# Chunks 1 and 2 take their four tiles as one group of 512 columns in the second mixer, its first matrix a pair ahead, and the planner counts port waits in the tails

## The chip, the core and the metric

The kernel runs on one core of one Trainium2 chip. The metric is the time of the whole kernel on the device, in microseconds (us). Before the change three runs gave 1989.48, 1990.63 and 1990.86 us; the median is 1990.63 us.

The engines are named here as the profile names them: PE is TensorE (PEld its weight loads), DVE is VectorE, ACT is ScalarE, POOL is GpSimd, SP is the engine that issues most of the DMAs.

## The reference, cut to what matters

One sequence of S = 2048 rows, D = 512 columns, H = 32 heads, F = 1792 hidden columns.

```python
mod = silu(c) @ w_mod                      # six rows of 512: sa, ca, ga, sb, cb, gb
h = layernorm(x) * (1 + ca) + sa
x = x + ga * attention(h, wqkv, wo)        # 32 heads of 16 columns
h = layernorm(x) * (1 + cb) + sb
# block B on h:
u = gelu(layernorm(h) @ w1)                # shifted by +1, -1, +2, -2 rows, a quarter of the columns each
x1 = h + shifted(u) @ w2                   # first mixer, across rows
B = x1 + gelu(layernorm(x1) @ w3) @ w4     # second mixer, across columns
out = x + gb * B
```

## The kernel before

The work is cut into four **chunks** of 512 rows, each of four **tiles** of 128 rows. First come the weights and q, k and v, then the attention, chunk by chunk, which takes three quarters of the time. After it, or between its last steps for chunk 0, each chunk runs a **tail**: the output projection `wo`, two layer norms, `w1` with GELU, `w2` with the row shift, another layer norm, and then the second mixer, `w3` with GELU and `w4`.

Every fp32 product is made of three matmuls: each operand is split into a high part and a low part, and high x high, high x low and low x high are added in PSUM (lines 356, 358, 360). A block of 128 output columns of `w3` thus takes 4 x 3 = 12 matmuls, whose moving side is as wide as the group of rows that they serve. A tile of `w4` takes 3 matmuls of 512 columns for each 128 hidden columns.

**Groups.** The shift by up to two rows means that a chunk can finish its `w2` only for rows whose followers are there, so that chunk 0 carries three tiles into the second mixer, chunks 1 and 2 the last tile of the chunk before and three of their own, and chunk 3 five. The list `sub` holds these tiles in groups. Chunk 0 has one group of three tiles (384 columns), chunks 1 and 2 have two groups of two (256 columns each), chunk 3 has a group of two and a group of three.

**Plans.** `PLAN` says in which order the pieces of `w3` and `w4` come. In `PAIRS` (chunk 0) a piece is 256 hidden columns, called a pair, and `w3` runs one pair ahead of `w4`. In the other plan (chunks 1 to 3) `w3` takes four blocks of 128 columns, then `w4` takes the same four.

**Weights.** Each piece of 1 MB holds both parts of the split weights. Chunk 0 builds the pieces of `w3` and `w4` itself (`fresh`, lines 1217 to 1219): a piece is loaded raw in two halves; POOL multiplies it by `gb` (`w4` alone), ACT rounds the high part, DVE subtracts for the low part (`wr<-raw,wr`). It is stored to DRAM, and later chunks load it back (`wr<-Ws`). A `Ring` gives out a few buffers in order.

**Order.** The whole program is one list of instructions per engine, written in the order in which a planner issues them. `Sched` keeps a clock for each engine; a chain of operations on ACT, DVE and POOL is put on these clocks by its costs (`cA`, `cD`, `cG` for 512 columns and so on), and generators (`tail`, `rest` for the second mixer, `norm_T` for the transposes of a normalised group) give their matmuls to PE when the planner's clock says that what they need is ready. Generators earlier in the list go first: the tails of chunks 1 to 3 stand before the second mixers. On the chip each engine then follows its own list strictly, so an instruction that is issued too early holds up what stands behind it.

The names in the profile: `xT` is a bank of transposes, from `osb` (attention output), `xf` (normalised for `w1` in chunks 1 to 3) or `xn` (the same in chunk 0, and normalised for `w3` in all chunks); `A` holds the split transposes; `g` the GELU results; `sq` the buffer between GELU and its split; `trs` the reciprocal root that POOL computes for a layer norm; `x` and `xb`/`xbs` the tiles of the residual. `w<-A,wr` is `w1` or `w3`, `w<-wr,g` is `w2` or `w4`.

Of the kernel before, what the change touches and what calls it, by code (L numbers as in the profile page):

```python
# [8 lines left out]
F32 = mybir.dt.float32  # L9
# [6 lines left out]
OP = mybir.AluOpType  # L16
# [5 lines left out]
P = 128  # L22
# [3 lines left out]
NC = S // CH  # L26
# [79 lines left out]
XB = 4  # L106


class Sched:
# [41 lines left out]
    def put(self, e, cost, ready, fn):  # L151
        self.end = self.T[e] = max(self.T[e], ready) + cost
        fn()
        return self.end
# [164 lines left out]
def cD(n=CH):  # L319
    return n / 0.96 + 69  # L320
# [7 lines left out]
def kernel(ctx, tc, A_x, A_wqkv, A_wo, B_w1, B_w2, B_w3, B_w4, c, w_mod, out):  # L328
# [869 lines left out]
    def fresh(w, i, key):  # L1198
        nm = pieces[i][0]
        left = [2]  # L1200

        def one(f):
            raw.append(f)
            left[0] -= 1
            if not left[0]:
                done.add(key)
                sch.dma(dma.dma_start, Ws[i], w.bitcast(F32))
                if len(made) == len(order["w3"] + order["w4"]) and len(raw) == NRAW:
                    raw.clear()
                    rings["r"].add([0])  # L1210
        for c in range(2):
            yield lambda: (i, c) in loadedq
            f, e = loadedq.pop((i, c))
            hi, lo = [w[:, h, 512 * c:512 * c + 512] for h in range(2)]
            ops = []
            if nm == "w4":
                ops.append(("G", cG(), lambda f=f: pool.tensor_tensor(f, f, gbrow, op=OP.mult)))
            sch.chain(*ops, ("A", cA(), lambda f=f, hi=hi: act.activation(hi, f, AF.Copy)),
                      ("D", cD(), lambda f=f, hi=hi, lo=lo: dve.tensor_tensor(lo, f, hi, op=OP.subtract)),
                      (None, 0, partial(one, f)), ready=e, prio=FPRIO)  # L1220
# [6 lines left out]
    PLAN = [PAIRS, [(nm, i, f0, nf) for i, (f0, nf) in enumerate(FG) for nm in ("w3", "w4")]]  # L1227
# [63 lines left out]
    def tail(ci):  # L1291
# [3 lines left out]
        if ci > 1:  # L1295
            yield lambda: ("w1", ci - 1) in done
# [71 lines left out]
        def ln_apply(dst, src, rs, mv):  # L1368
            return ("D", cD(), lambda: dve.tensor_scalar(dst, src, mv[:, 0:1], rs[:, 0:1], op0=OP.subtract, op1=OP.mult))
# [27 lines left out]
        def norm_T(ts, key, i):  # L1397
# [4 lines left out]
            xlive[xtag(key, ts[0])] -= len(ts)  # L1402

        for i, t in enumerate(new):
# [21 lines left out]
            go = partial(sch.chain, ("D", cD(), x1_add), ("D", 1050 + 750, center), ("D", 750, scale), *ops2,  # L1426
# [6 lines left out]
        def gelu(b, n, hi, lo, key):  # L1433
# [3 lines left out]
            sq = fa.tile([P, 3 * P], F32, name="sq", tag="sq", bufs=XB)[:, :n]  # L1437
# [63 lines left out]
        w, more = ring.get(2)  # L1501
        for si, ts in enumerate(sub):
            yield lambda: all(("g", ci, i, n) in done for i in range(1 + (t0 + 1 in ts)) for n in range(4))
            for t in ts:
# [10 lines left out]
                z = (("D", cD(), lambda xb=xb: dve.tensor_tensor(xb, xb, gbrow, op=OP.mult)),  # L1515
# [6 lines left out]
        if ci == 0:  # L1522
            rings["r"] = Ring(MIXER[0] + MIXER[1] * (NC - 1), rings["0"].spare)
            yield lambda: "C" in done
        sch.add(rest(ci, sub, An, gelu, wait_bank, tG))

    def rest(ci, sub, An, gelu, wait_bank, tG):
# [3 lines left out]
        plan = PLAN[ci > 0]  # L1531
        g2 = {}
        for nm, fi, f0, nf in plan:
# [3 lines left out]
            if nm == "w3":  # L1537
                g2[fi] = [tG(si, len(ts) * P, fi % 2 * nf if not ci else 0) for si, ts in enumerate(sub)]
# [202 lines left out]
```

## Time and profile before

| what | value |
|---|---|
| median of three runs | 1990.63 us |
| the profiled execution, its own time | 1992.18 us |
| its span (first to last instruction) | 1990.4 us |
| PE busy | 1934.7 us, 97% |
| DVE, ACT, POOL busy | 79%, 73%, 77% |
| attention ends, tails alone from | about 1509 us |
| chunk 0 done with its second mixer | about 1657 us |
| chunk 1, chunk 2, chunk 3 done | about 1772, 1889 and 1987 us |

Busy PE is the time in which at least one matmul was under way; a matmul of 512 columns is shown as 0.39 us long though the next one starts 0.23 us after it. How fast PE works is therefore read from the starts of a row of matmuls, and where it loses time from the column of idle time before an instruction, which names who ended it.

### The profile page before, as it was taken

The numbers are of one execution on the slowest core, as the hardware profiler recorded it, in microseconds if no ns is written. First come the engines' busy times: TensorE is split into PE (matmuls) and PEld (weight loads), VectorE is DVE, ScalarE is ACT, GpSimd is POOL, SyncE is SP. The second block draws the span as 40 slices with busy tenths as digits, with TensorE's granted clock in tenths as the row PEclk, the third lists the DMA queues.
The fourth block names the chain that finished last, engine by engine and source line by source line (L and its number), as shares of the span: only waits on it lengthen the run. The fifth ranks groups of instructions, "written<-read, shape, count | busy, mean of one in ns | idle before, by whom it ended". The sixth has DMA issues, their size and how long they took to land.

```text
span 1990.4 us, 41169 instructions
## 1 busy us (share of the span) xinstructions
PE 1934.7 (97%) x14456; PEld 1160.1 (58%) x14456; DVE 1579.6 (79%) x2763; ACT 1453.7 (73%) x2940; POOL 1535.6 (77%) x1404
## 2 busy tenths in 40 slices
PE   7999999999999999999999999999999989999999
PEld 5755554554444444444444444444457879898998
DVE  6398888888999999999999999999976784425211
ACT  6438887778999999999999999999975423232222
POOL 6339998889999999999999999999994653334222
PEclk9989999999999999999999999999999999999999
DMA  8777666454534353535353535364514766553541
GB/s 292 236 197 189 155 175 185 126 136 125 104 73 109 73 109 73 109 73 109 73 108 74 109 73 109 73 162 104 107 40 176 287 226 251 220 199 123 204 150 69
DMA packets 185502, 277.95 MB, mean 140 GB/s; under 512 B 117104, under 2 KB 127856, under 8 KB 169008
## 3 DMA queue, kind: packets, MB, share of 16 engines
q1 hardware_dynamic: 181792, 267.20, 49.5%
q10 hardware_dynamic: 2304, 4.20, 0.6%
q0 software_dynamic: 1200, 3.93, 0.5%
q8 instruction: 114, 1.87, 0.4%
q14 instruction: 92, 0.75, 0.1%
HBM read 211.81 MB, written 62.91 MB: 138 GB/s over the span
## 4 chain that ended last, share of the span: by engine, by line
PE 75%; DVE 13%; ACT 4%; issue 3%; DMA 3%; POOL 2%; SPq 0%; ACTq 0%; POOLq 0%; DVEq 0%
PE mb L992 17%; PE sc L1019 12%; PE pv L1093 11%; DVE mx L988 10%; PE w L356 6%; PE w L360 6%; PE w L358 6%; PE pv L1090 5%; PE ot L1120 3%; ACT pt L1015 3%; DMA wst<-in_A_wqkv_dram 1%; PE xT L1254 1%; POOL pt L1068 1%; DMA wr<-Ws 1%; PE q L360 1%
## 5 line engine op out<-in xcount | busy, mean ns | idle before, releaser
L988 DVE TENSOR_REDUCE mx<-mb 128x1 f32<-128x512 f32 x2048 | 1250.5, 681 | 57.0 <-PE mb L992 51.8
L1068 POOL TENSOR_SCALAR pt<-pt 128x1024 f16<-128x1024 uint16 x772 | 1017.0, 1368 | 67.3 <-ACT pt L1015 66.4
L1015 ACT ACTIVATE pt<-sc 128x512 int32<-128x512 f32 x1688 | 890.4, 623 | 94.7 <-PE mb L992 70.7
L992 PE MATMUL mb<-kst,qtl 62*128 62x512 f32 x2048 | 785.4, 463 | 17.4 <-ACT pt L1015 8.6
L1019 PE MATMUL sc<-qtl,kst 64*128 64x512 f32 x2048 | 744.0, 450 | 2.8 <-DVE mx L988 1.8
L992 PEld LDWEIGHTS mb<-kst,qtl 62*128 62x128 f32 x2048 | 361.6, 193 | 260.4 <-ACT pt L1015 137.8
L1019 PEld LDWEIGHTS sc<-qtl,kst 64*128 64x128 f32 x2048 | 337.3, 185 | 188.4 <-DVE mx L988 118.3
L1093 PE MATMUL pv<-pt,vst 128*32 128x512 f16 x3376 | 318.0, 395 | 3.6 <-ACT ac L1110 3.6
L1453 POOL TENSOR_TENSOR g<-sq,g 128x256 fp32r<-128x256 f32 (+1 forms) x120 | 95.3, 796 | 178.1 <-ACT g L1452 169.8
L1450 ACT ACTIVATE sq<-w 128x256 f32<-128x256 f32 (+1 forms) x126 | 51.4, 408 | 236.5 <-PE w L360 235.6
L1068 POOL TENSOR_SCALAR xbs<-xbs 128x1024 f16<-128x1024 uint16 x165 | 219.3, 1362 | 4.5 <-ACT xbs L1015 4.5
L1015 ACT ACTIVATE xbs<-sc 128x512 int32<-128x512 f32 x360 | 199.9, 642 | 10.9 <-PE mb L992 8.5
L1093 PEld LDWEIGHTS <-vst 128*32 128x32 bf16 x4096 | 91.2, 94 | 180.8 <-issue 162.0
L1560 DVE TENSOR_TENSOR x<-x,w 128x512 f32<-128x512 f32 x73 | 49.7, 684 | 156.7 <-PE w L360 156.7
L1090 PE MATMUL pv<-pt,vst 128*32 128x512 f16 (+1 forms) x1688 | 172.1, 391 | 1.6 <-POOL pt L1068 1.6
L358 PE MATMUL w<-A,wr 128*128 128x256 f32 (+1 forms) x520 | 155.1, 298 | 1.1 <-DVE A L346 1.0
L356 PE MATMUL w<-A,wr 128*128 128x256 f32 (+1 forms) x520 | 155.5, 299 | 0.2 <-DMA wr<-Ws 0.2
L360 PE MATMUL w<-A,wr 128*128 128x256 f32 (+1 forms) x520 | 154.6, 298 | 0.0
L356 PE MATMUL w<-wr,g 128*128 128x512 f32 x270 | 106.6, 395 | 2.0 <-DMA wr<-Ws 2.0
L358 PE MATMUL w<-wr,g 128*128 128x512 f32 x270 | 106.3, 394 | 0.0
L360 PE MATMUL w<-wr,g 128*128 128x512 f32 x270 | 106.2, 393 | 0.0
L358 PEld LDWEIGHTS w<-A,wr 128*128 128x128 f32 x520 | 100.2, 193 | 3.0 <-DVE A L346 2.1
(173 smaller groups left out, 2295.9 us busy)
## 6 DMA issues: line engine op xcount, KB each, us to landing
wr<-Ws SPq DMA_DIRECT2D x66, 1024.0 KB, 5.5
vst<-Vs SPq DMA_DIRECT2D x64, 768.0 KB, 5.2
kst<-Ks SPq DMA_DIRECT2D x126, 384.0 KB, 6.0
Ws<-wr SPq DMA_DIRECT2D x14, 1024.0 KB, 5.2
qtl<-Qs SPq DMA_DIRECT2D x128, 96.0 KB, 4.1
Vs<-vt SPq DMA_DIRECT2D x32, 384.0 KB, 4.3
Ks<-qk SPq DMA_DIRECT2D x16, 512.0 KB, 4.1
Qs<-qk SPq DMA_DIRECT2D x16, 512.0 KB, 3.0
```

Of the source, the lines that this page charges most:

```text
L356: te.matmul(o, lh, rh, start=first, stop=False)
L358: te.matmul(o, lh, rl, start=False, stop=False)
L360: te.matmul(o, ll, rh, start=False, stop=last)
L988: end = sch.crit("D", 605, e + PX, lambda: dve.reduce_max(mxs[u][:, j, g, c:c + 1], b, axis=AX.X))
L992: return ready, lambda: te.matmul(b, lhs, kst[u % 3][r, c * CH:(c + 1) * CH], start=True, stop=True), after
L1015: ea = sch.crit("A", 480, e + PX, lambda: act.activation(pt[s][:, j], b, AF.Exp))
L1019: return ready, lambda: te.matmul(b, kst[u % 3][r, kt * P:(kt + 1) * P], qst[u][r], start=True, stop=True), after
L1068: e_low[s] = XP["G"] + sch.crit("G", 1345, ready, lambda: pool.tensor_scalar(o, i, 0.5, 1.0, op0=OP.mult, op1=OP.mult))
L1090: te.matmul(acc[r:r + n, :], v[:, kt + i, c:c + n].bitcast(F16), pt[s + i].bitcast(F16)[:, j, 0::2], start=False, stop=kt == NKT - 2, skip ...
L1093: te.matmul(acc[r:r + 32, :], v[:, kt, r:r + 32], pt[s].bitcast(F16)[:, j, 1::2], start=kt == 0, stop=False, skip_group_check=True)
L1120: te.matmul(b[:, t * n:(t + 1) * n], ac[:, t * P:(t + 1) * P], smat.rearrange("p j d -> p (j d)"), start=True, stop=True)
L1453: ("G", cG(n), lambda: pool.tensor_tensor(lo, sq, hi, op=OP.subtract)), (None, 0, end), bank=b)
```

## The change

- `sub` for chunks 1 and 2 is one group of four tiles, so that a block of `w3` is 12 matmuls of 512 columns; each group is transposed when all four of its tiles are normalised.
- `PLAN` gives chunks 1 and 2 the order `PAIRS`; chunk 3 keeps its plan.
- The buffers between a GELU and its split (`sq`) become 512 columns wide, and three in number where there were four.
- The tail of a chunk after the first starts when the chunk before it has taken its `w2` pieces and two pieces wait in the ring, where it started at the end of the `w1` of that chunk.
- Costs of some DVE operations with SBUF operands (`Shared`: the low part of fresh weights, the two steps of a layer norm, the multiplication by `gb`) are put on the DVE clock behind the last POOL operation, if that started before them.

```diff
-XB = 4
+XB = 3
+class Shared(float):
+    pass
...
     def put(self, e, cost, ready, fn):
-        self.end = self.T[e] = max(self.T[e], ready) + cost
+        t = max(self.T[e], ready)
+        if e == "G":
+            self.busyG = t, t + cost
+        elif isinstance(cost, Shared) and self.busyG[0] <= t:
+            t = max(t, self.busyG[1])
+        self.end = self.T[e] = t + cost
...
-                      ("D", cD(), lambda f=f, hi=hi, lo=lo: dve.tensor_tensor(lo, f, hi, op=OP.subtract)),
+                      ("D", Shared(cD()), lambda f=f, hi=hi, lo=lo: dve.tensor_tensor(lo, f, hi, op=OP.subtract)),
...
-    PLAN = [PAIRS, [(nm, i, f0, nf) for i, (f0, nf) in enumerate(FG) for nm in ("w3", "w4")]]
+    PLAN = [PAIRS] * (NC - 1) + [[(nm, i, f0, nf) for i, (f0, nf) in enumerate(FG) for nm in ("w3", "w4")]]
...
         if ci > 1:
-            yield lambda: ("w1", ci - 1) in done
+            yield lambda: ("w2w", ci - 1) in done and len(rings["f"].q) >= 2
...
-            sub = [[t0 - 1, t0], new[1:3 + end]]
+            sub = [[t0 - 1, t0], new[1:3 + end]] if end else [[t0 - 1] + new[:3]]
...
-            return "x4" if ci and t in sub[0] else "xn"
+            return "x4" if ci and t in sub[0][:2] else "xn"
...
-            go = partial(sch.chain, ("D", cD(), x1_add), ("D", 1050 + 750, center), ("D", 750, scale), *ops2,
+            go = partial(sch.chain, ("D", cD(), x1_add), ("D", Shared(1050 + 750), center), ("D", Shared(750), scale), *ops2,
...
-            sq = fa.tile([P, 3 * P], F32, name="sq", tag="sq", bufs=XB)[:, :n]
+            sq = fa.tile([P, 4 * P], F32, name="sq", tag="sq", bufs=XB)[:, :n]
...
-        plan = PLAN[ci > 0]
+        plan = PLAN[ci]
```

Up to the last steps of the attention the instructions stand as before on PE. From there they are in another order, and three places show how.

The first is PE's list where chunk 2 goes from `w1` to `w2`, before:

```order
L356 MATMUL w1_26257<-A_24576,wr_26040 128x256
L358 MATMUL w1_26257<-A_24576,wr_26040 128x256
L360 MATMUL w1_26257<-A_24576,wr_26040 128x256
L356 MATMUL w2_26276<-wr_26042,g1_24441 128x512
L358 MATMUL w2_26276<-wr_26042,g1_24441 128x512
```

and now (the `w3` is that of chunk 1):

```order
L370 MATMUL w1_26199<-A_24525,wr_25985 128x256
L368 MATMUL w3_26140<-A_7629,wr_25847 128x512
L370 MATMUL w3_26140<-A_7629,wr_25847 128x512
L366 MATMUL w3_26140<-A_7629,wr_25847 128x512
L368 MATMUL w3_26140<-A_7629,wr_25847 128x512
L370 MATMUL w3_26140<-A_7629,wr_25847 128x512
L366 MATMUL w3_26227<-A_7629,wr_25847 128x512
L368 MATMUL w3_26227<-A_7629,wr_25847 128x512
L370 MATMUL w3_26227<-A_7629,wr_25847 128x512
L366 MATMUL w2_26233<-wr_25987,g1_24464 128x512
L368 MATMUL w2_26233<-wr_25987,g1_24464 128x512
```

Eight matmuls of `w3`, 512 columns wide, now stand between the last of `w1` and the first of `w2`.

The second place is PE's list where chunk 0's tiles, normalised for `w3`, are transposed (`xT<-ident,xn`), before:

```order
L360 MATMUL wo_24828<-wr_24580,A_24576 128x512
L1254 MATMUL xT_24858<-ident_64,xn_7631 128x128 x3
L1254 MATMUL xT_24863<-ident_64,xn_7631 128x128 x3
L1254 MATMUL xT_24870<-ident_64,xn_7631 128x128 x3
L1254 MATMUL xT_24876<-ident_64,xn_7631 128x128 x3
L356 MATMUL w3_24889<-A_7629,wr_24775 128x384
L358 MATMUL w3_24889<-A_7629,wr_24775 128x384
```

and now:

```order
L370 MATMUL wo_24872<-wr_24529,A_24525 128x512
L1264 MATMUL xT_24914<-ident_64,xn_7631 128x128 x3
L1264 MATMUL xT_24927<-ident_64,xn_7631 128x128 x3
L1264 MATMUL xT_24935<-ident_64,xn_7631 128x128 x3
L1264 MATMUL xT_24942<-ident_64,xn_7631 128x128 x3
L366 MATMUL w1_24960<-A_24525,wr_24612 128x256
L368 MATMUL w1_24960<-A_24525,wr_24612 128x256
```

Chunk 0's `w3` followed the transposes; now the `w1` of chunk 1 does. Between the `w2` of chunk 0 and the `w2` of chunk 1 stood 93 matmuls of `w3` and 36 of `w4` of chunk 0, and now stand 38 and none; the others follow later.

The third place is DVE's list up to the second `xf` of chunk 2, which the transposes of that chunk's first two tiles need, before:

```order
L1421 SCALAR_TENSOR_TENSOR xbs_7630<-x1_25445,tmv_25591,cbrow_77 128x512
L1424 SCALAR_TENSOR_TENSOR xbs_7630<-xbs_7630,trs_25592,sbrow_62 128x512
L367 BN_STATS tst_25593<-xbs_7630 128x6
L368 BN_AGGR tmv_25594<-tst_25593 128x2
L1361 TENSOR_SCALAR tmv_25594<-tmv_25594 128x1
L1560 TENSOR_TENSOR x1_22200<-x1_22200,w4_25705 128x512
L1219 TENSOR_TENSOR wr_25660<-raw_23997,wr_25660 128x512
L1369 TENSOR_SCALAR xf_7632<-xbs_7630,tmv_25594,trs_25595 128x512
```

and now:

```order
L1432 SCALAR_TENSOR_TENSOR xbs_7630<-x1_25280,tmv_25415,cbrow_77 128x512
L1572 TENSOR_TENSOR x1_22202<-x1_22202,w4_25479 128x512
L1572 TENSOR_TENSOR x1_22552<-x1_22552,w4_25498 128x512
L1435 SCALAR_TENSOR_TENSOR xbs_7630<-xbs_7630,trs_25416,sbrow_62 128x512
L1229 TENSOR_TENSOR wr_25507<-raw_23997,wr_25507 128x512
L377 BN_STATS tst_25417<-xbs_7630 128x6
L378 BN_AGGR tmv_25418<-tst_25417 128x2
L1371 TENSOR_SCALAR tmv_25418<-tmv_25418 128x1
L1572 TENSOR_TENSOR x1_22200<-x1_22200,w4_25547 128x512
L1229 TENSOR_TENSOR wr_25546<-raw_23997,wr_25546 128x512
L1229 TENSOR_TENSOR wr_25507<-raw_23997,wr_25507 128x512
L1379 TENSOR_SCALAR xf_7632<-xbs_7630,tmv_25418,trs_25419 128x512
```

Two subtractions for fresh weights and additions of `w4` results have moved in front of this `xf`.

## Rows read from the trace of the kernel before

**Rows 1.** The head of the page: the span.
```profile
span 1990.4 us, 41169 instructions
```
**Rows 2.** Windows; stretch: length, then busy by engine, clock, DMA share, GB/s.
```profile
1514.07:1593.30 79.23, 74.28 (x415) 66.61 (x415) 55.38 (x97) 34.08 (x70) 39.06 (x43) 0.94 0.73 266
1593.30:1656.80 63.50, 55.84 (x272) 48.86 (x273) 51.38 (x80) 18.93 (x36) 32.09 (x29) 0.95 0.70 253
1656.80:1764.20 107.40, 106.88 (x686) 96.91 (x685) 39.08 (x73) 31.34 (x76) 39.54 (x55) 1.00 0.57 210
```
**Rows 3.** Timeline of PE, chunk 1's mixer: start, length, engine, line, operation.
```profile
1713.39 0.27 PE L356 MATMUL w<-A,wr 128*128 128x256 f32 x1
...
1724.77 0.28 PE L360 MATMUL w<-A,wr 128*128 128x256 f32 x1
1724.89 0.39 PE L356 MATMUL w<-wr,g 128*128 128x512 f32 x1
...
1735.65 0.39 PE L360 MATMUL w<-wr,g 128*128 128x512 f32 x1
```
**Rows 4.** Timeline of PE: the first weights of `w2`, chunks 2 and 3.
```profile
1692.38 0.40 PE L360 MATMUL w<-wr,g 128*128 128x512 f32 x1
1693.30 0.50 PE L356 MATMUL w<-wr,g 128*128 128x512 f32 x1 [0.52 <-DMA wr<-Ws]
...
1817.40 0.50 PE L356 MATMUL w<-wr,g 128*128 128x512 f32 x1 [0.58 <-DMA wr<-Ws]
```
**Rows 5.** Groups by line, 1600 to the end: count, busy us, mean ns.
```profile
L1560 DVE TENSOR_TENSOR x<-x,w 128x512 f32<-128x512 f32 x67 | 45.6, 685 | 156.5 <-PE w L360 156.4
L1453 POOL TENSOR_TENSOR g<-sq,g 128x384 fp32r<-128x384 f32 x15 | 16.2, 1079 | 17.2 <-ACT g L1452 13.4 <-issue 3.8
```
**Rows 6.** Waits of PE, 1510 to 1660: total us, times, longest.
```profile
PE xT L1254 <- DVE xf L1369: 8.6, 3, 7.2
PE xT L1254 <- DVE sq L1444: 1.8, 1, 1.8
PE xT L1254 <- DVE xn L1369: 1.8, 1, 1.8
PE w L358 <- DVE A L346: 1.0, 2, 0.7
```
**Rows 7.** Timeline of PE: the longest of these waits.
```profile
1639.54 1.76 PE L1254 MATMUL xT<-ident,xf 128*128 128x128 f32 x7 [7.20 <-DVE xf L1369]
```
**Rows 8.** Timeline of DVE and POOL: a DVE operation beside POOL, and others alone.
```profile
1560.60 1.28 POOL L1217 TENSOR_TENSOR raw<-raw,gbrow 128x512 f32<-128x512 f32 x1
1560.68 1.48 DVE L1369 TENSOR_SCALAR xf<-xb,tmv,trs 128x512 f32<-128x512 f32 x1
1562.09 0.68 DVE L1219 TENSOR_TENSOR wr<-raw,wr 128x512 fp32r<-128x512 f32 x1
...
1564.29 0.54 DVE L1369 TENSOR_SCALAR xf<-xb,tmv,trs 128x512 f32<-128x512 f32 x1
```
**Rows 9.** Groups by line on DVE, 1514.07 to 1656.8: count, busy us, mean ns.
```profile
L1219 DVE TENSOR_TENSOR wr<-raw,wr 128x512 fp32r<-128x512 f32 x28 | 26.0, 942 | 0.4 <-ACT wr L1218 0.3
L1424 DVE SCALAR_TENSOR_TENSOR xb<-xb,trs,sbrow 128x512 f32<-128x512 f32 x4 | 4.8, 1194 | 0.0
L1369 DVE TENSOR_SCALAR xf<-xb,tmv,trs 128x512 f32<-128x512 f32 x4 | 3.4, 854 | 0.7 <-POOL trs L1364 0.7
L1424 DVE SCALAR_TENSOR_TENSOR xbs<-xbs,trs,sbrow 128x512 f32<-128x512 f32 x2 | 3.2, 1590 | 0.4 <-POOL trs L1364 0.4
L1369 DVE TENSOR_SCALAR xf<-xbs,tmv,trs 128x512 f32<-128x512 f32 x2 | 2.6, 1323 | 0.0
```
**Rows 10.** Windows: stretches at half clock (the clock stands third from the end).
```profile
1514.70:1518.00 3.30, 3.30 (x18) 3.30 (x17) 1.58 (x4) 2.16 (x5) 0.00 (x0) 0.50 0.99 413
1545.40:1552.20 6.80, 6.31 (x19) 5.80 (x20) 6.66 (x15) 1.65 (x3) 3.77 (x4) 0.50 0.75 261
1637.60:1644.30 6.70, 4.76 (x18) 4.76 (x19) 5.51 (x8) 2.34 (x4) 3.01 (x2) 0.50 0.82 289
```

More of the change, by code (lines that the diff above doesn't have):

```diff
@@ L120, in __init__ @@
         self.end = 0.0
+        self.busyG = 0.0, 0.0
         self.gapmin = GAPMIN
@@ L1368, in ln_apply @@
         def ln_apply(dst, src, rs, mv):
-            return ("D", cD(), lambda: dve.tensor_scalar(dst, src, mv[:, 0:1], rs[:, 0:1], op0=OP.subtract, op1=OP.mult))
+            return ("D", Shared(cD()), lambda: dve.tensor_scalar(dst, src, mv[:, 0:1], rs[:, 0:1], op0=OP.subtract, op1=OP.mult))
         def later(key, fn):
@@ L1401, in norm_T @@
             yield from transposed(lambda k, j: xn[key, ts[j]][:, k * P:(k + 1) * P], range(KT), len(ts), A)
-            xlive[xtag(key, ts[0])] -= len(ts)
+            for t in ts:
+                xlive[xtag(key, t)] -= 1
         for i, t in enumerate(new):
@@ L1501, in tail @@
         w, more = ring.get(2)
+        done.add(("w2w", ci))
         for si, ts in enumerate(sub):
@@ L1514, in tail @@
                 r, m, ops = ln_ops(xb)
-                z = (("D", cD(), lambda xb=xb: dve.tensor_tensor(xb, xb, gbrow, op=OP.mult)),
+                z = (("D", Shared(cD()), lambda xb=xb: dve.tensor_tensor(xb, xb, gbrow, op=OP.mult)),
                      ("G", cG(), lambda xb=xb, x1=x1: pool.tensor_tensor(x1, x1, xb, op=OP.add)), mark(("z", t)))
@@ L1522, in tail @@
         if ci == 0:
-            rings["r"] = Ring(MIXER[0] + MIXER[1] * (NC - 1), rings["0"].spare)
+            rings["r"] = Ring(sum(MIXER, []), rings["0"].spare)
             yield lambda: "C" in done
@@ L1537, in rest @@
             if nm == "w3":
-                g2[fi] = [tG(si, len(ts) * P, fi % 2 * nf if not ci else 0) for si, ts in enumerate(sub)]
+                g2[fi] = [tG(si, len(ts) * P, fi % 2 * nf if plan is PAIRS else 0) for si, ts in enumerate(sub)]
                 for si, ts in enumerate(sub):
```

## The prediction

> **What bounds the kernel now.** I read the page first, then the windows by stage, then the timeline of PE (TensorE), and last what PE waited for. The span is 1990.4 us [rows 1], the profiled execution took 1992.18 us, and the median of the runs is 1990.63 us. My sum is made against the profiled execution, and the forecast is set against the median, 1.55 us lower. Up to the last steps of the attention PE's list is unchanged, so that only the time from about 1500 us on can change.
>
> There, two stages differ. While chunk 0 is in its tail and second mixer (1514.07 to 1656.8), the windows show PE idle for 5.0 us of 79.2 and 7.7 us of 63.5, and the clock at 0.94 and 0.95, while VectorE is busy for 55.4 and 51.4 us [rows 2]. In the mixer of chunk 1 the clock is 1.00 and PE is idle for 0.5 us of 107.4 [rows 2]. So in chunks 1 to 3 a matmul less is time saved, and in chunk 0 what counts is what PE waits for: VectorE, for 8.6 + 1.8 + 1.8 + 1.0 = 13.2 us [rows 6]. The longest wait, 7.2 us, is that of the transposes for chunk 2 [rows 7].
>
> **Wider matmuls in chunks 1 and 2.** 96 matmuls of 256 columns start from 1713.39 to 1724.77, 95 steps, 0.1198 us each; 48 of 512 columns from 1724.89 to 1735.65, 47 steps, 0.2289 us each [rows 3]. In each of the two chunks `w3` has 14 blocks x 12 matmuls x 2 groups = 336 of 256 columns; now 168 of 512. Over both, 672 x 0.1198 = 80.5 us become 336 x 0.2289 = 76.9 us: **-3.6 us**, and no other engine covers it, since PE sets the pace there. As bounds for the new shape I take the rows of the same width in `w4` and a tenth either way of the gain: -4.0 to -3.2.
>
> The Trainium skill, "TensorE: Matmul & The Clock Gate", section "Back-to-back issue gap", gives a fixed 2.5 ns for each matmul on top of its columns; 336 matmuls fewer would be worth 0.84 us by that, an estimate from the page. The rows give 2 x 119.8 - 228.9 = 10.7 ns for the second matmul, and I keep them.
>
> What else goes with it costs nothing. The plan in pairs adds 3 more turns of `w4` in each chunk over 4 tiles, 24 additions of 0.685 us [rows 5] or 16.4 us of VectorE over two chunks; VectorE has 39 us of work in 107 [rows 2], and each addition stands beside the 6 matmuls (1.37 us) of the next tile. The GELU of a block is now 512 wide: POOL took 1.08 us for 384 [rows 5], so some 1.4 us for 512, against 12 x 0.229 = 2.75 us in which PE makes the next block. Three buffers hold 8.2 us of blocks; that one buffer is gone is not felt while a chain takes less than that. Without this cover POOL would set the pace, which is far off.
>
> **A DMA wait that is covered.** The first `w2` of chunk 2 starts 0.92 us after the matmul before it, where 0.23 is the rule: it waits 0.69 us for its weights [rows 4]. Now eight `w3` matmuls, 1.83 us, stand in front: **-0.7 us**. The like wait in chunk 3 [rows 4] stays, as its `w2` still follows `w1` directly. Bounds -0.7 and 0.
>
> **Chunk 0 in another order.** PE's work here is the same; it is cut differently. 55 `w3` and 36 `w4` matmuls, about 17.8 us, move from before the `w2` of chunk 1 to behind it. I go through the waits, first with VectorE as slow as now. 384 columns I price at 0.174 us, halfway between the two steps above.
> - First transposes after the attention: 1.8 us [rows 6]. The normalised tile now stands behind splits of the other transposes, two to four operations of about 0.68 [rows 8], with 11 matmuls of `wo` in front: 1.8 to 4.5, I take 2.9.
> - Transposes of chunk 0 for `w3`, and the split after them: 1.8 + 1.0 [rows 6]. In front stood 28 matmuls of `wo` after the last `w2`, now 20, that is 1.8 us less cover: 4.6, at most 6.5 with the operations that have moved in front on VectorE.
> - First transposes for chunk 1: 1.4 (the 8.6 less the 7.2). PE's cover goes from 60 `w3` and 18 `w4` (14.6 us) to 48 `w1` and 16 `w3` (8.5 us); VectorE's list loses 3 subtractions for weights, 2 statistics, a centring, a scaling and 2 additions, some 7.6 us. Depending on whether PE runs at half clock there, 0 to 4.1; I take 2.3.
> - Transposes for chunk 2: 7.2 [rows 7]. VectorE's list from the second addition of `wo` to the `xf` gains 2 subtractions (0.94 each [rows 9]) and an addition, +2.6; PE's cover goes from 36 `w4` and 38 `w3` to 37 and 49, +2.1: 7.7.
>
> That makes 17.5 us against 13.2. Now the planner's new rule. Beside a POOL operation that ends at 1561.88, an `xf` takes 1.48 us; alone it takes 0.54, and a subtraction 0.68 [rows 8]. Over the stage the subtractions lose 28 x 0.26 = 7.3 us in this way, `xf` 2.8 and the scaling (against 0.68) 3.9: 14.0 us [rows 9]. If the planner's clock knows all of it, it gives the transposes to PE later, with other matmuls in front; if it knows nothing, all stays. It counts VectorE behind the last POOL operation, and not POOL behind VectorE, so I take half, 7 us: 10.5 us against 13.2, **-2.7 us**, with +4.3 and -9.7 as ends. Last, 24 matmuls of `w1` (2.9 us) that stood between the last steps of the attention now follow it: +0.5, from 0 to 2.9.
>
> The Trainium skill, "SBUF — State Buffer", section "Who interferes with whom", has VectorE and GpSimd share a pair of ports as an exclusive lock: whoever starts first holds it to the end of the instruction. Rows 8 agree for VectorE's side. By that rule POOL is late as often, which the planner's rule leaves out; this speaks for the second rival.
>
> **Sum.** -3.6 - 0.7 - 2.7 + 0.5 = -6.5 us: 1985.7 for an execution like the profiled one, **1984.1** for the median.
>
> **The rivals.**
> 1. *The waits nearly go.* With all 14 us known to the planner the waits are 3.5 us: -3.6 - 0.7 - 9.7 + 0.5 = -13.5, or 1977.1; one of the spells at half clock, 6.8 us long [rows 10], would go with them, 3.4 us more: 1973.7. I put it at 1975.5. For it: VectorE is busy for 107 of 143 us [rows 2], so that there is room. Against it: all four waits stand behind long runs of VectorE work, where there is nothing else to give to PE. Chance 0.20.
> 2. *The planner's rule changes nothing on the chip* and the 17.5 us stay: -3.6 - 0.7 + 4.3 + 0.5 = +0.5, or 1991.1, no change that can be told. For it: the counts of VectorE's list above. Chance 0.22.
> 3. *Slower: VectorE becomes the bound of the first stretch and PE's clock falls.* The first stretch loses 17.8 us of PE's work, and with it the cover. After each of three waits the clock fell to 0.50, for 3.3 to 6.8 us [rows 10], 1.2 in place of 2.4 GHz. Four waits of 2.9 to 7.7 us in place of two long ones would bring two more spells of 6.8 us, 3.4 us each where PE sets the pace: 1991.1 + 6.8 = 1997.9. It decides as soon as the waits pass some 17 us and two of the spells fall on stretches without a VectorE wait behind them. Against it: a slow PE shortens the next wait. Chance 0.14.
> 4. *The wide matmul gains what the page says,* 0.8 us in place of 3.6: 1986.9. The rows are against it. Chance 0.04.
>
> **Chances.** The forecast has 0.40, with 1981 to 1987.5 as its own range. A measurement of this kernel tells some 0.2%, 4 us, from no change. Faster by more than that, below 1986.65: 0.85 of the forecast, rival 1 and a part of rival 4, 0.55. Slower, above 1994.6: nearly all of rival 3, 0.13. The rest, 0.32. The range that leaves out 2 in 10 runs from the middle of rival 1 to the lower part of rival 3: 1975.5 to 1995.
>
> **What would show it.** In the profile after, a block of `w3` in chunks 1 and 2 starts every 12 x 0.229 = 2.75 us, and the two chunks together from the end of chunk 0 to the last `w4` of chunk 2 are 4.3 us shorter. No DMA wait stands before the `w2` of chunk 2. PE's waits for VectorE from 1510 us to the end of chunk 0 sum to about 10.5 us; over 15 says rival 2, under 6 rival 1. Windows at clock 0.50 of more than 17 us in sum say rival 3. I am wrong in the first term if the steps of 512 columns with a GELU behind them are over 0.24 us, for then POOL or the buffers hold PE; and in the third if a wait of over 2 us turns up in chunks 1 to 3, where the group of four has to be complete before its transposes.

## The result and the profile after

The changed kernel takes 1994.65 us (median of 16 runs, 1991.47 to 1997.08) against 1990.69 us before: a ratio of 1.0018, 95% interval 1.0011 to 1.0024, so slower by about 4 us where 6.5 us less was forecast. One of the eleven runs of m4, an experiment below, took 3650.62 us; its ratio leaves that run out, and without it its median is 1992.8 us. First the head of the page of the changed kernel, which answers to [rows 1], then its windows by stage, cut at the first `w2` matmul of chunk 1 and at the end of chunk 0, with the columns of [rows 2]; the last two lines are the first stretch of the kernel before with the same cut, and a part of the first stretch of the changed kernel.

```profile
span 1993.2 us, 40424 instructions
```
```profile
1511.90:1584.40 72.50, 60.53 (x342) 54.83 (x343) 46.50 (x90) 26.10 (x57) 30.81 (x38) 0.88 0.54 197
1584.40:1664.10 79.70, 74.52 (x370) 65.48 (x370) 58.91 (x94) 28.29 (x54) 44.01 (x38) 0.98 0.77 282
1664.10:1768.00 103.90, 103.90 (x522) 87.82 (x521) 47.84 (x86) 28.74 (x54) 39.33 (x42) 1.00 0.60 225
...
1514.07:1591.30 77.23, 72.73 (x410) 65.67 (x410) 55.38 (x97) 33.28 (x68) 37.98 (x42) 0.93 0.72 262
...
1549.00:1567.00 18.00, 14.23 (x89) 13.33 (x87) 17.58 (x33) 5.26 (x14) 11.82 (x14) 0.91 0.82 306
```

The first stretch lost 17.8 us of `w3` and `w4` matmuls and took in 24 of `w1` (2.9 us), and became only 4.7 us shorter than the same stretch before (77.2 us): PE is idle for 12.0 of 72.5 us, at a clock of 0.88. VectorE is busy for 46.5 of the 72.5 us, but unevenly: from 1549 to 1567 us, around one of the longest waits below, it is busy for 17.58 of 18.00 us (in the kernel before for 17.59 of the same 18). Over the stretch it is no bound; there it is. Chunk 0 ends at 1664.26 instead of 1656.94, and from there to the last matmul it takes 4.5 us less than before. The whole loss lies ahead of 1664 us, and the expected gain behind it is there.

Next the timeline of PE in chunk 1's mixer (the first and the last of 24 `w3` matmuls) and in chunk 3, which answer to [rows 3, 4], and the group of the low part of the wide GELU on GpSimd from 1600 us on [rows 5].

```profile
1736.01 0.39 PE L366 MATMUL w<-A,wr 128*128 128x512 f32 x1
...
1741.22 0.39 PE L370 MATMUL w<-A,wr 128*128 128x512 f32 x1
...
1822.30 0.50 PE L366 MATMUL w<-wr,g 128*128 128x512 f32 x1 [0.53 <-DMA wr<-Ws]
```
```profile
L1464 POOL TENSOR_TENSOR g<-sq,g 128x512 fp32r<-128x512 f32 x28 | 36.9, 1319 | 64.6 <-ACT g L1463 52.3 <-issue 11.2 <-POOL trs L1374 1.0
```

23 steps in 5.21 us are 0.2265 us each; over all 336 such matmuls the mean is 0.2278. The 0.53 us at 1822.30, in chunk 3, is the only wait of PE behind 1664 us that the waits list; that of chunk 2's `w2` is gone. Now PE's waits from 1510 to 1665 us, which answer to [rows 6], and the larger ones singly in PE's timeline [rows 7], where a count of transposes ends with the window that was read.

```profile
PE xT L1264 <- DVE xf L1379: 8.1, 3, 4.2
PE xT L1264 <- DVE xn L1379: 6.0, 2, 3.8
PE wo L366 <- issue: 2.1, 1, 2.1
PE w L366 <- DVE sq L1455: 1.8, 1, 1.8
PE w L366 <- DMA wr<-Ws: 1.0, 1, 1.0
```
```profile
1516.36 1.91 PE L1264 MATMUL xT<-ident,osb 128*128 128x128 f32 x16
1520.38 0.47 PE L366 MATMUL wo<-wr,A 128*128 128x512 f32 x1 [2.10 <-issue]
...
1525.78 0.97 PE L1264 MATMUL xT<-ident,xn 128*128 128x128 f32 x5 [2.19 <-DVE xn L1379]
...
1555.89 0.87 PE L1264 MATMUL xT<-ident,xn 128*128 128x128 f32 x6 [3.77 <-DVE xn L1379]
...
1568.93 0.30 PE L1264 MATMUL xT<-ident,xf 128*128 128x128 f32 x1 [1.74 <-DVE xf L1379]
1571.36 1.54 PE L1264 MATMUL xT<-ident,xf 128*128 128x128 f32 x6 [2.13 <-DVE xf L1379]
...
1631.07 0.98 PE L1264 MATMUL xT<-ident,xf 128*128 128x128 f32 x7 [4.19 <-DVE xf L1379]
```

Before, one wait of 7.2 us [rows 7] stood above others of at most 1.8 [rows 6]; now there are six of 1.7 to 4.2. The longest but one, at 1555.89, is read from VectorE's timeline, here from the last `w2` result of the tile on:

```profile
1549.49 0.67 DVE L1523 TENSOR_TENSOR xbs<-xbs,w 128x512 f32<-128x512 f32 x1
1550.09 2.48 DVE L1229 TENSOR_TENSOR wr<-raw,wr 128x512 fp32r<-128x512 f32 x4
1552.50 0.67 DVE L1423 TENSOR_TENSOR x<-x,wo 128x512 f32<-128x512 f32 x1
1553.10 0.68 DVE L377 BATCH_NORM_STATS2 tst<-xbs 128x6 f32<-128x512 f32 x1
...
1555.29 0.54 DVE L1379 TENSOR_SCALAR xn<-xbs,tmv,trs 128x512 f32<-128x512 f32 x1
```

Four subtractions for weights and an addition stand between the tile's result and its statistics. The stretches at half clock, as in [rows 10], are now five and sum to 19.8 us there against 16.8:

```profile
1512.60:1515.90 3.30, 3.30 (x18) 3.30 (x17) 1.21 (x4) 1.24 (x1) 0.99 (x1) 0.50 1.00 420
1526.30:1529.60 3.30, 3.30 (x12) 2.72 (x11) 2.42 (x4) 1.20 (x2) 0.00 (x0) 0.50 0.00 0
1557.00:1560.30 3.30, 3.30 (x17) 3.30 (x16) 3.16 (x4) 2.50 (x6) 3.30 (x4) 0.50 1.08 447
1570.70:1577.30 6.60, 5.94 (x23) 5.94 (x24) 2.48 (x4) 2.72 (x6) 1.46 (x2) 0.50 0.07 25
1632.10:1635.40 3.30, 3.30 (x12) 3.30 (x12) 2.51 (x5) 1.16 (x3) 1.80 (x1) 0.50 1.02 387
```

VectorE's losses beside GpSimd did fall, as these groups show beside [rows 9]:

```profile
L1229 DVE TENSOR_TENSOR wr<-raw,wr 128x512 fp32r<-128x512 f32 x28 | 22.8, 835 | 4.8 <-ACT wr L1228 4.3
...
L1435 DVE SCALAR_TENSOR_TENSOR xb<-xb,trs,sbrow 128x512 f32<-128x512 f32 x4 | 3.9, 985 | 0.9 <-POOL trs L1374 0.9
...
L1435 DVE SCALAR_TENSOR_TENSOR xbs<-xbs,trs,sbrow 128x512 f32<-128x512 f32 x3 | 3.0, 984 | 0.0
...
L1379 DVE TENSOR_SCALAR xf<-xb,tmv,trs 128x512 f32<-128x512 f32 x4 | 2.8, 697 | 3.4 <-POOL trs L1374 3.4
...
L1379 DVE TENSOR_SCALAR xf<-xbs,tmv,trs 128x512 f32<-128x512 f32 x2 | 2.6, 1318 | 0.0
```

Over 0.68 for a subtraction or scaling and 0.54 for an `xf`, that is 4.3 + 2.1 + 2.2 = 8.6 us, where it was 14.0.

### The profile page after: what moved, and what is told of

Same layout as the page of the kernel before. It is cut to its first block, busy times and chain, and to the rows that moved or that the text cites. A ratio compares the mean times of both kernels' runs of the same rounds, so it can differ in the third digit from the quotient of the medians.

```text
span 1993.2 us, 40424 instructions
## 1 busy us (share of the span) xinstructions
PE 1932.9 (97%) x14120; PEld 1143.8 (57%) x14120; DVE 1587.8 (80%) x2781; ACT 1443.8 (72%) x2883; POOL 1533.9 (77%) x1377
## 4 chain that ended last, share of the span: by engine, by line
PE 74%; DVE 13%; ACT 4%; issue 3%; POOL 2%; DMA 2%; SPq 0%; ACTq 0%; POOLq 0%; DVEq 0%
PE mb L1002 17%; PE sc L1029 12%; PE pv L1103 11%; DVE mx L998 10%; PE w L366 6%; PE w L368 6%; PE w L370 6%; PE pv L1100 5%; PE ot L1130 3%; ACT pt L1025 3%; DMA wst<-in_A_wqkv_dram 1%; POOL pt L1078 1%; PE xT L1264 1%; PE v L366 1%; PE v L368 1%
## 5 line engine op out<-in xcount | busy, mean ns | idle before, releaser
L1002 PE MATMUL mb<-kst,qtl 62*128 62x512 f32 x2048 | 786.3, 463 | 17.9 <-ACT pt L1025 8.6
L1461 ACT ACTIVATE sq<-w 128x256 f32<-128x256 f32 (+2 forms) x100 | 47.4, 474 | 262.0 <-PE w L370 213.9
L1464 POOL TENSOR_TENSOR g<-sq,g 128x256 fp32r<-128x256 f32 (+2 forms) x94 | 91.6, 976 | 170.0 <-ACT g L1463 153.3
L1572 DVE TENSOR_TENSOR x<-x,w 128x512 f32<-128x512 f32 x97 | 65.8, 684 | 144.4 <-PE w L370 144.3
L366 PE MATMUL w<-A,wr 128*128 128x256 f32 (+2 forms) x408 | 136.3, 334 | 1.8 <-DVE sq L1455 1.8
L370 PE MATMUL w<-A,wr 128*128 128x256 f32 (+2 forms) x408 | 136.3, 334 | 0.0
L368 PE MATMUL w<-A,wr 128*128 128x256 f32 (+2 forms) x408 | 136.3, 334 | 0.0
L163 ACT ACTIVATE pt<-pt 128x1024 f16<-128x1024 uint16 x73 | 101.9, 1395 | 0.0
```

Of the source, the lines that this page charges most:

```text
L366: te.matmul(o, lh, rh, start=first, stop=False)
L368: te.matmul(o, lh, rl, start=False, stop=False)
L370: te.matmul(o, ll, rh, start=False, stop=last)
L1002: return ready, lambda: te.matmul(b, lhs, kst[u % 3][r, c * CH:(c + 1) * CH], start=True, stop=True), after
L1464: ("G", cG(n), lambda: pool.tensor_tensor(lo, sq, hi, op=OP.subtract)), (None, 0, end), bank=b)
```

## The experiments

**How they are read.** Beside the time, one sum for each kernel from its trace: the stretch from the attention's last output transposes to the last `w4` of chunk 0, in which each step from one matmul's start to the next is split into its work (0.229, 0.174 and 0.120 us for 512, 384 and 256 columns, 0.128 for a transpose), a wait (over 0.35 us beyond it), and a rest, most of it the slow clock. Executions with the same order reach this stretch 3 to 5 us apart, so times are compared by medians and this sum only says where. "New order" is that of the changed kernel; it has 2.8 us more work in the stretch because 24 `w1` matmuls now follow the attention. Empty fields were not worked out.

| kernel | median us | ratio to before (95%) | stretch | work | waits | rest |
|---|---|---|---|---|---|---|
| before | 1990.7 | | 147.7 | 125.8 | 15.7 | 6.1 |
| changed | 1994.65 | 1.0018 (1.0011-1.0024) | 157.2 | 128.5 | 20.2 | 8.3 |
| e1 no rule | 1988.4 | 0.9990 (0.9982-0.9999) | 149.0 | 125.6 | 18.4 | 4.6 |
| e2 rule alone | 1997.2 | 1.0036 (1.0024-1.0048) | 155.5 | 128.6 | 20.0 | 6.7 |
| e3 three buffers alone | 1995.2 | 1.0021 (1.0012-1.0029) | 150.1 | 125.8 | 20.4 | 3.8 |
| e5 groups, old plan | 2001.4 | 1.0053 (1.0041-1.0065) | | | | |
| e6 pairs, two groups | 1993.5 | 1.0016 (1.0007-1.0025) | 150.9 | 125.8 | 20.3 | 4.6 |
| b1 slots 4, then 3 | 1986.6 | 0.9977 (0.9967-0.9986) | 145.2 | 125.6 | 14.2 | 5.1 |
| m1 first x1 by SyncE | 1996.5 | 1.0032 (1.0020-1.0045) | 158.1 | 128.5 | 21.1 | 8.2 |
| m4 later x1 by SyncE | 1992.9 | 1.0008 (0.9999-1.0017) | 154.7 | 128.5 | 17.9 | 7.9 |
| m2 new order, no scale | 1986.9 | 0.9979 (0.9970-0.9988) | 150.0 | 128.5 | 15.7 | 5.4 |
| m3 before, no scale | 1981.5 | 0.9953 (0.9940-0.9965) | 137.1 | 125.8 | 8.0 | 3.1 |
| m5 splits on GpSimd | 1995.1 | 1.0021 (1.0012-1.0030) | 158.0 | 128.5 | 21.1 | 8.1 |
| m7 new order, no split | 1985.4 | 0.9968 (0.9956-0.9981) | 146.8 | 128.5 | 14.2 | 3.9 |
| m8 before, no split | 1976.4 | 0.9923 (0.9909-0.9937) | 132.4 | 125.8 | 5.1 | 1.3 |
| b3 scale on VectorE | 1980.7 | 0.9950 (0.9938-0.9963) | | | | |
| m9 b3 with the rule | 1984.4 | 0.9963 (0.9951-0.9976) | 146.5 | 128.5 | 15.6 | 2.1 |
| b4 b3 and x1 by SyncE | 1979.6 | 0.9936 (0.9923-0.9948) | | | | |

**Which part of the change costs it.**

e1, the changed kernel with the rule off:
```diff
-        elif isinstance(cost, Shared) and self.busyG[0] <= t:
+        elif False:
```


> The changed kernel with the planner's port rule switched off and all else of the change kept (groups of four, pairs, the new start of a tail, three GELU buffers). The theory: the rule alone reorders chunk 0, and that reorder costs the 7.3 us by which chunk 0's last w4 came later in the changed kernel (1664.26 against 1656.94), while the rest of the change gains 4.5 us after it. Then chunk 0 ends near 1657 again, the time is 1990.7 - 4.5 = about 1986.2 us, a ratio to the kernel before of 0.9977, and TensorE's waits that are named after VectorE between 1505 and 1665 us are back near 13 us from 16. Rival A, the three GELU buffers or the wider groups hold chunk 0 back: about 1994.6 us, ratio 1.002, and chunk 0 still ends near 1664. Rival B, the loss is spread over rule and buffers: between, about 1990 us.

e2, the kernel before with the rule alone (four buffers of 384 columns, old plan, groups and start):


> The kernel before with the planner's port rule alone. The theory: chunk 0 runs as in the changed kernel and ends 7.3 us later than before, at about 1664; the later chunks stay as before, so 1990.7 + 7.3 = about 1998 us, ratio 1.0037. If a part of the 7.3 us is given back later (the changed kernel's order takes 91 matmuls of mixer 0 out of the first stretch, and the later chunks may wait less because their tails are further on) it is 1994 to 1998. Rival A, the buffers or groups do the harm: 1990.7 us, ratio 1.000, chunk 0 ends near 1657. As the prediction had the rule, at -2.7 us, it would be 1988.

e3, the kernel before with a buffer less:
```diff
-XB = 4
+XB = 3
```


> The kernel before with three GELU buffers instead of four and nothing else. The theory: no GELU wait stands on TensorE's path, so 1990.7 us within 1 us, ratio 1.000. Rival A: the third buffer is what chunk 0 lacks, chunk 0 ends 3 to 7 us later and the time is 1994 to 1998 us.

The rule alone costs 0.36% or some 6 us, and taking it out of the change gives 6.3 us back: the theory holds for it. But the first run stayed 2.2 us over its 1986.2, and three buffers alone, which should have cost nothing, cost 4.0. The number of buffers is a condition that the planner asks before it gives a `w3` or `w1` block to PE, and with three it sets chunk 0 in yet another order (from the first transposes after the attention on, equal in e1 and e3 for 434 matmuls). Both orders have 3 to 5 us more of waits than that of before. So rival A was half right: the buffer acts in chunk 0, through the planner. In the change it adds little to the rule's loss: with the rule on, PE's order is the same with four buffers (e2) as with three up to the wait at 1568.93, and the stretches are 155.5 and 157.2 us.

b1 keeps what is to gain, has the rule off as in e1, and gives PE its old order back in chunk 0's first stretch (behind the first `w2` of chunk 1 the order still differs):
```diff
-            sq = fa.tile([P, 4 * P], F32, name="sq", tag="sq", bufs=XB)[:, :n]
+            k = (me - XB[2]) % XB[0] * XB[1] * P      # XB = [4, 3, 0]
+            sq = sqs[:, k:k + n]                      # sqs: one tile of 12 * P
...
+        if ci == 1:                                   # in rest(), ahead of its plan
+            yield lambda: not live
+            XB[:] = 3, 4, gn[0]
```


> No port rule, groups of four, pairs and the new start of a tail; one buffer of 1536 columns that is cut into four GELU slots of 384 until chunk 1's second mixer begins and into three of 512 from there. The matmuls of chunk 0's first stretch then stand as in the kernel before. The runs so far give 4.0 us lost with three buffers alone and 2.9 us gained with three buffers, groups and pairs without the rule. The theory (any other order of chunk 0 than that of before costs 4 to 6 us; groups and pairs give back 4 to 7): 1990.9 - 5.5 = about 1985.5 us, ratio 0.997, below the 1988.4 us of the version with three buffers throughout. Rival (the three buffers cost something in chunks 1 to 3, not in chunk 0): 1988 us, the same as that version.

PE's waits in chunk 0 are those of [rows 6] again, up to the length of the longest:
```profile
PE xT L1264 <- DVE xf L1379: 7.8, 3, 6.0
PE xT L1264 <- DVE sq L1457: 1.8, 1, 1.8
PE xT L1264 <- DVE xn L1379: 1.8, 1, 1.8
PE w L368 <- DVE A L356: 1.0, 2, 0.7
```
4.2 us faster than before: with that stretch left as it was, groups, pairs and start bring about what the prediction's two first terms said, -4.3. That it is so near is partly luck, for by the traces 3.6 us of it lie behind chunk 0. b1 beats both kernels.

**What in the gain is width, and what the plan.** e5 is e1 with the old plan for chunks 1 and 2, e6 is e1 with the two groups. (What was expected of e6 speaks of the old start too; its edit leaves the new start in place.)
```diff
-    PLAN = [PAIRS] * (NC - 1) + [[... FG ...]]
+    PLAN = [PAIRS] + [[... FG ...]] * (NC - 1)
```


> As the first run of this set (no port rule), with chunks 1 and 2 as one group of four tiles but the old plan of their second mixer (four w3 blocks, then their w4 blocks). The theory: the 3.6 us of the wider matmuls stay and the w2 load stays covered; what the pairs add is the cover of the last GELU ahead of each w4 set, six sets with at most 1.5 us each where nothing else is ready. So 1986.2 us if other chains fill these places and up to 1986.2 + 9 = 1995 us if none do; the estimate is 1988, ratio 0.9986, and TensorE waits for ScalarE's GELU show in chunks 1 and 2. Rival: the pairs bring the gain, not the width, so without them the time is the 1990.7 us of before.


```diff
-            sub = [[t0 - 1, t0], new[1:3 + end]] if end else [[t0 - 1] + new[:3]]
+            sub = [[t0 - 1, t0], new[1:3 + end]]
```


> No port rule, three GELU buffers and the old start and the old two groups of two tiles, but the plan in pairs with its first matrix a pair ahead. The run with groups and the old plan took 2001.4 us and the one with both 1988.4. Theory (width gives 3.6 us, pairs only cover what the width uncovers): as three buffers alone, 1995 us, ratio 1.002. Rival (pairs are the gain by themselves): 1988 to 1990 us, with no wait for a GELU in chunks 1 and 2.

The groups without the pairs lose 13 us against e1, more than the bound of 9. The waits of e5 from 1655 us to the end:
```profile
PE xT L1264 <- DVE xf L1379: 6.3, 3, 3.1
PE w L370 <- POOL g L1464: 1.2, 4, 0.3
PE w L366 <- DMA wr<-Ws: 0.6, 1, 0.6
```
The GELU waits that I had priced are 1.2 us; the larger part are transposes of the next chunk, which had no waits behind 1660 us before, and behind each of the two longest PE runs at half clock for 3.4 us. The pairs with the new start are within the noise of three buffers alone (1993.5 against 1995.2).

One length in the traces settles this better than the whole time, because it hardly scatters: from the end of chunk 0 to the start of the last matmul it is 329.5 to 329.7 us in all six kernels with two groups (before, e2, e3, e6, m3, m8), 325.0 to 326.0 in all eleven with one group and the pairs, and 337.4 in e5. So pairs and start alone gain nothing there (e6, 329.5); the width is the gain, and the pairs are what lets it be had. What e2 and e3 lose, they lose ahead of it.

**What in the new order costs.** Here the order stays and one engine's work is taken away, or moved to another engine.

m1 was meant to take four issues off ScalarE ahead of the wait at 1520.38, but moved chunk 0's own loads:
```diff
-                act.dma_start(x1t[t], x_d[t * P:(t + 1) * P])      # in tail_load()
+                dma.dma_start(x1t[t], x_d[t * P:(t + 1) * P])
```


> The changed kernel in its own order, with the loads of x1 for the later chunks issued by SyncE instead of ScalarE. In the changed kernel four of these issues take ScalarE 2.23 us at 1516.7, ahead of the copies of A for which the projection's matmul at 1520.4 waits 2.25 us. Theory (chunk 0 loses 4.5 us of waits and 2.1 us of clock by the new order as a whole, each wait by its own chain): this one wait shrinks by about 2 us, 1994.65 - 2 = 1992.6 us, the other waits stay. Rival one (ScalarE's issues are the cause): the waits behind it fall too, 1990 us or less. Rival two (the wait is only passed on to the xn wait 2.34 us at 1525.8): 1994.6 us.

The four later issues stayed on ScalarE and took 4.42 us, where they had taken 2.23, and the wait of the projection rose with them; the first row is ScalarE's, the second PE's:
```profile
1519.83 4.42 ACTq L1321 DMA_DIRECT2D x<-in_A_x_dram  x4
```
```profile
1525.72 0.76 PE L366 MATMUL wo<-wr,A 128*128 128x512 f32 x1 [5.10 <-issue]
```
m4 moves the loads of the same line in `x1_loads()`, line 1321:


> The changed kernel in its own order, with the loads of x1 for chunks 1 to 3 issued by SyncE. (The earlier run of that intent moved chunk 0's own four loads instead; the four issues on ScalarE ahead of the copies of A stayed, took 4.42 us instead of 2.23, and the wait for them 5.24 instead of 2.25: the time rose 1.9 us.) If that wait is on the path: it goes, 1994.65 - 2 = 1992.6 us. If it is passed on to the next wait: 1994.6 us.

That wait is gone from the list, the others are what they were, and the time is 1.7 us less, as expected (the two intervals overlap, so the gain is not clear of the noise). It is one of six.

m2 and m3 leave out GpSimd's scaling in the new and in the old order, m7 and m8 VectorE's subtractions (a copy on ScalarE stands in their place); m5 moves the latter to GpSimd in m2:
```diff
-                ops.append(("G", cG(), lambda f=f: pool.tensor_tensor(f, f, gbrow, op=OP.mult)))
+                ops.append(("G", cG(), lambda: None))                                    # m2, m3, m5
...
-                      ("D", ..., lambda f=f, hi=hi, lo=lo: dve.tensor_tensor(lo, f, hi, op=OP.subtract)),
+                      ("D", ..., lambda f=f, hi=hi, lo=lo: act.activation(lo, f, AF.Copy)),   # m7, m8
+                      ("D", ..., lambda f=f, hi=hi, lo=lo: pool.tensor_tensor(lo, f, hi, op=OP.subtract)),   # m5
```


> The changed kernel in its own order, without GpSimd's scaling of the raw w4 weights (14 instructions of 1.48 us between 1505 and 1665 us, 20.6 us; the output lacks that scale). Rival (GpSimd's queue is the cause: rstd stands behind these and other instructions there, and VectorE's xn and xf behind rstd): the waits of 3.92 at 1555.9, 1.90 and 2.30 at 1569 to 1571 and 4.33 us at 1631 shrink by most, 1988 to 1991 us. Theory (order and VectorE's own queue, which has no idle time from 1549 to 1567): at most 1 to 2 us off, 1992.6 to 1994.6 us.

> The kernel before in its own order, without GpSimd's scaling of the raw w4 weights (14 instructions; the output lacks that scale): the control for the changed kernel without it, which took 1986.9 us, 7.8 us less than with it. Theory A (the new order of chunk 0 is hurt because it puts more behind GpSimd's queue): the kernel before gains less, 2 to 4 us, 1987 to 1989 us, and the two orders come out within 1 us of each other once the rest of the change (-4 to -6 us) is taken off: the changed kernel without the scaling is then still 4 us behind its share. Theory B (the scaling costs either order the same 7 to 8 us: before has one wait of 7.34 us behind xf at 1639.5): 1983 us, and GpSimd's queue doesn't explain the difference between the two orders.

> The changed kernel in its own order, without the scaling of the raw w4 weights, and with their subtraction for the low part moved from VectorE to GpSimd (28 instructions of 0.69 us off VectorE, about as many of 1.4 us onto GpSimd, the output lacks the scale). Theory (the 3.92 us wait for xn at 1556 is VectorE's own queue: four such subtractions, 2.48 us, and two adds stand ahead of xn there): that wait falls to about 1.5 us and the half clock behind it with it, so 1984 us if GpSimd's longer queue takes nothing back. Rival (xn is late because of what comes before VectorE): the wait stays at 3.9 us, and the time is the 1986.9 us of the run without the scaling or, with GpSimd's queue full again, up to 1994 us.

> The changed kernel in its own order, with VectorE's 28 subtractions for the low part of the raw weights (0.69 us each) replaced by a second copy on ScalarE (0.63 us), which has idle time there; the low part is then left out and the output wrong by it. Theory one (the new order sets these subtractions ahead of the normalisations that TensorE waits for: four of them, 2.48 us, stand ahead of the statistics of xn at 1550 to 1552.5): the 3.92 us wait for xn falls to about 1.5 and the time by 3 to 5 us, 1990 to 1992 us, and the kernel before with the same edit gains less than 2 us. Theory two (the chain from the last w2 result over statistics, rstd and xn to TensorE is too long for the work that the new order leaves to cover it, whatever stands between): the wait falls by less than 1 us and the time by 0 to 2 us.

> The control for the run ahead of it: the kernel before in its own order with the same subtractions replaced by copies on ScalarE. Theory one (they hurt the new order alone): 1989 to 1991 us. Theory two: it gains the same as the changed kernel, within 2 us.

m2 alone looked like proof that GpSimd's queue is the cause: 7.8 us. Its control takes that back, since the old order gains 9.9, as much or more. m5 gave no answer on VectorE: on GpSimd the four subtractions stand ahead of the `trs` that the same `xn` needs, for 5.77 us, and the wait of 3.77 us came out at 4.48:
```profile
1548.54 5.77 POOL L1229 TENSOR_TENSOR wr<-raw,wr 128x512 fp32r<-128x512 f32 x4 [0.75 <-ACT wr L1228]
1554.26 1.26 POOL L1528 TENSOR_TENSOR x<-x,xbs 128x512 f32<-128x512 f32 x1
1555.47 0.75 POOL L1484 CAST g<-g 128x260 fp32r<-128x260 f32 x2
1556.18 0.55 POOL L1374 TENSOR_TENSOR trs<-tmv,mhalf 128x1 f32<-128x1 f32 x1
```
m7 does answer for that wait, which falls from 3.77 us to 1.37:
```profile
1553.04 1.31 PE L1264 MATMUL xT<-ident,xn 128*128 128x128 f32 x10 [1.37 <-DVE xn L1379]
```
But m8 gains 15.4 us where m7 gains 9.3. Theory one explains a wait and not the difference between the orders. With the subtractions away, PE's waits from 1510 us to the end of chunk 0 in the new order (m7, first) and in the old (m8) are:
```profile
PE w L366 <- DMA wr<-Ws: 4.5, 2, 2.7
PE xT L1264 <- DVE xn L1379: 3.6, 2, 2.2
PE wo L366 <- issue: 2.0, 1, 2.0
PE w L366 <- DVE sq L1455: 1.8, 1, 1.8
PE xT L1264 <- DVE xf L1379: 1.1, 1, 1.1
```
```profile
PE xT L1254 <- DVE sq L1444: 1.8, 1, 1.8
PE w L356 <- DMA wr<-Ws: 1.1, 1, 1.1
PE xT L1254 <- DVE xf L1369: 0.9, 1, 0.9
PE w L358 <- DVE A L346: 0.6, 1, 0.6
```
Relieve VectorE, and the old order has nearly no waits, while the new one keeps those of `wo`, `xn` and the weights.

**The rule on a better version.** b3 is b1 with the scaling on VectorE, m9 puts the rule back on it, b4 is b3 with m4's edit:
```diff
-                ops.append(("G", cG(), lambda f=f: pool.tensor_tensor(f, f, gbrow, op=OP.mult)))
+                ops.append(("D", cD(), lambda f=f: dve.tensor_tensor(f, f, gbrow, op=OP.mult)))
```


> The best version so far (no port rule, four GELU slots in chunk 0 and three wide ones after it, groups and pairs, 1986.6 us) with the scaling of the raw w4 weights on VectorE instead of GpSimd, which also lets the planner order chunk 0 anew. If GpSimd's queue is what the waits for xf hang on (6.20 us at 1640.6 in that version): 14 x 1.40 us off GpSimd for 14 x 0.68 us on VectorE, the wait goes by most, 1982 to 1984 us. If a new order costs what the other two did: 1990 us.

> The best version so far (1980.7 us) with the port rule put back and nothing else. If the order that the rule makes is what costs, whatever GpSimd carries: 1980.7 + 6 = about 1987 us. If it costs only because GpSimd's queue is full in that order: 1981 to 1983 us.

> The best version so far (1980.7 us: no port rule, four GELU slots in chunk 0, groups and pairs, the raw scaling on VectorE) with the loads of x1 for chunks 1 to 3 issued by SyncE. In the changed kernel that edit took the 2.25 us wait of the projection away and gave 1.7 us. Here those loads stand beside a 1.99 us wait behind VectorE's sq at 1513.5, whose chain begins with ScalarE's square: 1979 to 1981 us.

b3 is 10 us faster than the kernel before. With the rule it loses 3.6 us, between the two expectations. That a part of the rule's loss hangs on GpSimd would fit, but isn't shown: the intervals of b3 and m9 overlap, and behind the wait at 1568.93 the order of m9 is another than that of the changed kernel. b4 is the fastest, 0.9936, but its 1.1 us over b3 lie within the intervals.

## Why the prediction was wrong

**The wider matmuls** (-3.6) **and the DMA wait** (-0.7) were right: from the end of chunk 0 to the last `w4` of chunk 2 it is 226.8 us (1664.26 to 1891.10) against 231.7, 4.8 less where 4.3 were forecast, and b1 is 4.2 us faster. That also rules out rival 4. A `w3` block takes 12 x 0.2265 = 2.72 us, and GpSimd's 1.32 us for the wide GELU lie beside it. That the plan in pairs only costs free additions was too little said: without it the same groups lose 13 us (e5).

**"Three buffers ... not felt"** holds in chunks 1 and 2. In chunk 0 e3 shows 4.0 us through the planner; the prediction didn't ask what else reads that number.

**The waits of chunk 0 with VectorE as slow as now**, 17.5 us, came out well in sum: 15.9 named after VectorE and the 2.1 of the projection, 18.0. That is partly luck. The first item, 2.9, came out at 6.1: 1.8 before a `w1` matmul at 1511.90, 2.1 at the projection behind ScalarE's issues, which I did not see, and 2.2 at 1525.78, the normalised tile that the item describes. Then come 3.8 for `xn` (4.6), 3.9 for chunk 1's `xf` (2.3) and 4.2 for chunk 2's (7.7).

**"I take half, 7 us"** is the step that failed. VectorE's losses beside GpSimd did fall, by 14.0 - 8.6 = 5.4 us, near that half. But PE's waits rose, by 4.5 us in the table, and the rule alone makes the kernel 6.0 us slower (e2). I took a microsecond that VectorE saves for one that PE waits less. As far as the rows show, the saved time went into VectorE's own waits: the subtractions and `xf` now have 4.3 and 3.4 us of idle time before them, where it was 0.3 or 0.4 and 0.7 [rows 9]. That none of it reached PE isn't shown, since the 17.5 us are an estimate. So the term is +4.5 and not -2.7, near the +4.3 of rival 2.

**The half clock**, priced only in rival 3, is most of the rest in the table, which grew by 2.2 us. The 24 `w1` matmuls came out as forecast: the stretch starts 2.2 us earlier and has 2.8 us more work, 0.6 in all. With the 4.5 us gained behind chunk 0 this makes -4.5 + 4.5 + 2.2 + 0.6 = 2.8 us, by which the two profiled spans differ; the medians differ by 4.0, and single executions scatter by as much. By the prediction's own tests the waits of 15.9 us (over 15) point to rival 2 and the 19.8 us at half clock (over 17) to rival 3, though the kernel before already had 16.8 [rows 10], of which the last 6.7 began inside a wait and not after it; the time, 4.0 us over before, lies between the two. Rival 3's reason holds in part: VectorE became no bound of the stretch as a whole, but it is one from 1549 to 1567 us, where it was as busy before. The cover that the stretch lost is less than the 17.8 us of that rival, since 24 `w1` matmuls came in.

**Why the new order has more waits** is shown in part. Shown is that it is the order (e1, e2), that neither GpSimd's scaling nor VectorE's subtractions account for the difference to the old one (m2 with m3, m7 with m8), and the cause of two waits: four issues on ScalarE ahead of the copies of `A` (m4), four subtractions ahead of a tile's statistics (m7). What is left I read, but did not test by adding matmuls: less PE work between a result and its use. The projection now follows its transposes directly, where 8 other transposes and 48 `w1` matmuls (6.2 us) stood; the transposes of `xn` at 1555.89 have 20 matmuls of `wo` in front and not 28. Why the planner's clock, which knows VectorE's losses better now, gives the worse order stays open. What it still leaves out is GpSimd's side (last section); a rule that counts both sides was not tried.

## What to carry to other kernels

An engine's saved time is not the path's: follow it to the instruction that the bound engine waits for before it enters a sum. A constant that a planner reads (a buffer count, a cost) can reorder work far from where it is meant, so compare orders wherever the number is asked, and keep the old order there if it waits less. Judge a suspected load in both orders: a relief that helps the new one may help the old one as much or more.

## What the runs showed of the hardware

Four load issues in a row on ScalarE took 2.23 us in one run and 4.42 in another with the same order on PE, and what stood behind them waited so much longer; why they differ was not tried. 28 subtractions of 0.94 us on average on VectorE, which is busy for three quarters of chunk 0, cost the whole kernel 15.4 us (m8), though no wait of PE is named after them: without them the waits in the table fall from 15.7 to 5.1 us, two of the three spells at half clock go, and the rest falls from 6.1 to 1.3 us.

GpSimd loses time beside VectorE too. Of its 14 scalings of raw weights in chunk 0 of the kernel before, seven took 1.27 to 1.31 us and seven took 1.42 to 1.73. In each of the slow seven a VectorE operation with all its inputs in SBUF had started first and ran on for 0.27 to 0.59 us; in the fast seven none such ran on for more than 0.16.
